# Score products of the first two head pairs from operands written in place, with a changed order of the start

## The chip, the cores and the metric
One NeuronCore of a Trainium2 chip runs one program. Its engines work in parallel, each in the order of its own queue: PE (matrix products; PEld is its weight load), DVE (vector), ACT (scalar and activation functions), POOL (GpSimd) and SP (which here only issues DMAs). The metric is the device time of one execution in microseconds (us); less is better.

## The reference, cut to what matters
The input is q, k, v of 4 batches x 8 heads x 576 positions x 64 values, and the weights of two feed-forward layers. The attention output (2304 rows of 512) goes through a layer of 8 experts, of which each row takes one, and then through a dense layer of 2048 hidden units.

```python
q_rot, k_rot = (rotate(q), rotate(k))
scores = scale * np.matmul(q_rot, k_rot.transpose(0, 1, 3, 2))
scores = scores - np.max(scores, axis=-1, keepdims=True)
attn = np.exp(scores)
attn = attn / (np.sum(attn, axis=-1, keepdims=True) + 1e-09)
return np.matmul(attn, v).astype(np.float32)
...
h = x @ w_in
r = np.maximum(h, 0.0)
g = r * r
return (g @ w_out).astype(np.float32)
```

## The kernel before, in words
**Stages.** `attention` takes the 32 heads as 16 pairs (P = 0 to 15); then come the experts and the dense layer. Two heads of 64 values fill the 128 partitions: head j of a pair lies on partitions 64j to 64j+63. A pair's q and k come in one load of 1.28 MB (`load`, L176, tile `qk`, two buffers, so the load of pair P+2 waits until the last reader of pair P's buffer is done). `rotate` (L189) turns them in place with three operations over 1280 columns: two products with tables (`times`, L392) and one sum (`plus`, L388). For pair 0 it is done in two halves, k (n = 0) and q (n = 1).

**Splitting.** The products run in a rounded 32-bit format, so each operand is split: `high` (L195) writes the rounded part `hi` on ACT, `low` (L202) the rest `lo` by a subtraction (on POOL unless told otherwise; `minus` is L384). Score = hi·hi + lo·hi + hi·lo. `stack_up` (L212) rearranges by DMA: for each head j, `kZ` holds the head's k high part twice, on both halves of the partitions, `qZ` holds its q high part above its q low part, and `QH[P % 2][j]` holds the q high part on the head's own partitions, with zeros on the other 64 (written once, L150). One product of `kZ` and `qZ` over 128 partitions then gives hi·hi + lo·hi.

**Scores.** A pair has nine score tiles s = 0 to 8, in the order 2, 8, 4, 1, 0, 5, 7, 3, 6. Tiles 0 to 7 are 128 queries of one head (j = s // 4) against 576 keys, in two halves u of 288 columns; tile 8 holds the last 64 queries of both heads. `scores` (L228) makes tiles 0 to 7 of 4 products (2 at L241, 2 at L243) and tile 8 of 6, into one of two PSUM buffers `ps`. `smax` (L250) takes the maximum on DVE, `sexp` (L253) the exponential and its sum on ACT, which frees the buffer. `turn` (L261) transposes the exponentials on PE into one of four buffers `pp`, `turned` (L278) copies them out on DVE or ACT, `values` (L296) multiplies with v, and `project` and `finish` scale and gather.

**Order.** The order of the work on every queue is written out by hand: `at(t, f)` puts a step into a heap under a planned time t, and the steps are issued in order of t, after all of `prepare` (L140). The planned times only order the queues; an engine waits for what it needs. The offsets `OFF` (L103) are added to 15.954 P. For pair 1 score 2 stands at 31.6, its exponential at 33.4 and score 4 at 34.7; for pair 0 exponentials 5, 7, 3 and 6 stand at 25.7, 26.4, 29.4 and 30.1. For pair 2 the three operations of `rotate` on POOL stand at 20.6, 23.6 and 26.5, `high` on ACT at 32.1, `low` on POOL at 33.6 and `stack_up` at 36.7; for pair 3 `load` stands at 21.9 and `rotate` at 36.6 to 42.4. `prepare` itself holds the loads, the clearing of buffers, all of pair 0's and pair 1's rotating and splitting, 16 products on PE that nobody reads (`warm`, L162), and both pairs' `stack_up`.

Of the kernel before, what the change touches and what calls it, by code (L numbers as in the profile page):

```python
# [10 lines left out]
F32 = mybir.dt.float32  # L11
F32R = mybir.dt.float32r
I32 = mybir.dt.int32
U32 = mybir.dt.uint32
AF = mybir.ActivationFunctionType
# [6 lines left out]
B, H, S, D = 4, 8, 576, 64  # L22
# [35 lines left out]
def shape_constants():  # L58
# [27 lines left out]
    for b in range(B):  # L86
        for c in range(4):
# [15 lines left out]
OFF = dict(pair=15.954, load=-26.0, v=8.0, rope=-11.279, hi=0.235, lo=1.675, z=4.815,  # L103
           S=[21.118, 20.135, 15.671, 27.85, 18.735, 24.184, 28.378, 24.712, 17.071],
           max=[21.846, 20.96, 16.399, 28.578, 19.463, 24.912, 29.183, 25.517, 18.084],
           exp=[22.666, 21.951, 17.479, 29.363, 20.248, 25.697, 30.078, 26.412, 18.869],
           un=[32.589, 32.153, 35.217, 38.036, 36.617, 23.748, 28.906, 37.6, 35.653, 34.253, 33.817],
           out=[33.418, 34.148, 36.917, 39.025, 37.411, 29.788, 32.958, 38.405, 36.294, 35.538, 34.643],
           av=[41.194, 44.969], x=[46.747, 47.789], pj=54.426, fin=58.03)
# [3 lines left out]
def attention(tc, rope, ident, qk, v, w_gate, xd, on_batch, later):  # L113
    nc = tc.nc
    stack = contextlib.ExitStack()
    pool = lambda name, **kw: stack.enter_context(tc.tile_pool(name=name, bufs=1, reuse_waits="tile", **kw))
    ldp, cp, wp = pool("ld"), pool("ac"), pool("aw")
# [7 lines left out]
    QH = [[cp.tile([128, 512], F32R, name=f"QH{i}{j}") for j in range(2)] for i in range(2)]  # L125

    SS = [cp.tile([128, 9, 2], F32, name=f"ss{i}") for i in range(6)]
    T = {}
    sched = []

    def at(t, f):
        heapq.heappush(sched, (round(t, 3), len(T["n"]), f))
        T["n"].append(0)
# [3 lines left out]
    def ppt(name, shape=(128, 512)):  # L137
        return psa.tile(list(shape), F32, name=name, tag="pp", bufs=4)

    def prepare():  # L140
        nc.scalar.dma_start(out=TB[:, :, 0], in_=rope)
        load(0)
        load(1)
        for t in Xs:
            nc.gpsimd.memset(t[:, 576:640], 0.0)
        for t in SS:
            nc.gpsimd.memset(t[:, :, 1:2], 1e-9)
        for two in QH:
            for j in range(2):
                nc.gpsimd.memset(two[j][64 - 64 * j:128 - 64 * j].bitcast(F32), 0.0)  # L150
        nc.gpsimd.memset(R, 0.0)
        for r in range(2):
            d = slice(64 * r, 64 * r + 64)
            nc.gpsimd.tensor_copy(R[d, :, r, 0:64], ident[d, d].unsqueeze(1).broadcast_to([64, 4, 64]))
        for o, lo, hi in ((0, 64, 640), (576, 0, 64)):
            nc.scalar.activation(TB[:, :, 1, o:o + hi - lo], TB[:, :, 0, lo:hi], AF.Copy, scale=0.125)
        for n in range(2):
            rotate(0, n, nc.vector)
            high(0, n)
        w = ppt("warm")  # L160
        for i in range(16):
            nc.tensor.matmul(w, T["hi", 0][:, 0, 0:128], T["hi", 0][:, 0, 0:512], start=True, stop=True)  # L162
        for n in range(2):
            low(0, n, nc.vector)
            stack_up(0, n)
        load(2)
        rotate(1, None, nc.vector)
        high(1)
        low(1)
        load_v(0)  # L170
        for r in range(2):
            nc.sync.dma_start(out=R[64 * r:64 * r + 64, :, r, 64:72], in_=w_gate.rearrange("(g r d) e -> r d g e", r=2, d=64)[r])
        later()
        stack_up(1)

    def load(P):  # L176
        t = T["qk", P] = ldp.tile([128, 2, 2, 640], F32, name="qk", tag="qk", bufs=2)
        src = qk[P].rearrange("p (w n c) -> p w n c", w=2, n=2)
        if P == 0:
            for n in range(2):  # L180
                nc.sync.dma_start(out=t[:, :, n], in_=src[:, :, n])
        else:
            nc.sync.dma_start(out=t, in_=src)

    def load_v(P):
        V = T["V", P] = ldp.tile([128, 2, 5, 64], F32, name="V", tag="V", bufs=2)
        nc.sync.dma_start(out=V, in_=v[P].rearrange("p (h c d) -> p h c d", h=2, c=5))

    def rotate(P, n, eng, step=None):  # L189
        x, a = T["qk", P], slice(0, 2) if n is None else slice(n, n + 1)  # L190
        for i, (f, o, y) in enumerate(((times, 0, TB[:, 0, a]), (times, 1, TB[:, 1, a]), (plus, 0, x[:, 1, a]))):
            if step in (None, i):
                f(eng, x[:, o, a], x[:, o, a], y)

    def high(P, n=None):  # L195

        if ("hi", P) not in T:
            T["hi", P] = wp.tile([128, 2, 640], F32R, name="XH", tag="XH", bufs=2)
        a = slice(0, 2) if n is None else slice(n, n + 1)
        nc.scalar.activation(T["hi", P][:, a], T["qk", P][:, 0, a], AF.Copy)  # L200

    def low(P, n=None, eng=None):  # L202
        if ("lo", P) not in T:
            T["lo", P] = wp.tile([128, 2, 640], F32R, name="XL", tag="XL", bufs=2)
        a = slice(0, 2) if n is None else slice(n, n + 1)
        args = T["lo", P][:, a], T["qk", P][:, 0, a], T["hi", P][:, a].bitcast(F32)
        if eng is None:
            nc.gpsimd.tensor_sub(*args)
        else:
            minus(eng, *args)  # L210

    def stack_up(P, n=None):  # L212

        h, l = T["hi", P].bitcast(F32), T["lo", P].bitcast(F32)
        for j in range(2):
            r = slice(64 * j, 64 * j + 64)
            q = nc.scalar if P == 0 and j == 1 else nc.sync
            if n != 1:
                Z = T["kZ", 2 * P + j] = wp.tile([128, 640], F32R, name="kZ", tag="kZ", bufs=4)
                for i in range(2):  # L220
                    q.dma_start(out=Z[64 * i:64 * i + 64].bitcast(F32), in_=h[r, 0])
            if n != 0:
                Z = T["qZ", 2 * P + j] = wp.tile([128, 640], F32R, name="qZ", tag="qZ", bufs=4)
                q.dma_start(out=Z[0:64].bitcast(F32), in_=h[r, 1])
                q.dma_start(out=QH[P % 2][j][r].bitcast(F32), in_=h[r, 1, 0:512])
                q.dma_start(out=Z[64:128].bitcast(F32), in_=l[r, 1])

    def scores(P, s):  # L228

        t = T["S", P, s] = ps.tile([128, 2, 512], F32, name="ps", tag="ps", bufs=2)  # L230
        if s < 8:
            j, c = divmod(s, 4)
            todo, qs, qh = [j], slice(c * 128, c * 128 + 128), QH[P % 2][j]
            qh = qh[:, qs]
        else:
            todo, qs, qh = [0, 1], slice(512, 640), T["hi", P][:, 1, 512:640]
        k0 = 0 if s in (4, 5, 6, 7) else 64
        for i, j in enumerate(todo):
            Q1, K1 = T["qZ", 2 * P + j], T["kZ", 2 * P + j]
            for u in range(2):  # L240
                nc.tensor.matmul(t[:, u, 0:288], Q1[:, qs], K1[:, k0 + 288 * u:k0 + 288 * u + 288], start=i == 0, stop=False)  # L241
        for u in range(2):
            nc.tensor.matmul(t[:, u, 0:288], qh, T["lo", P][:, 0, k0 + 288 * u:k0 + 288 * u + 288], start=False, stop=True)  # L243
# [98 lines left out]
    def route(P, t=None):  # L342
        t = OFF["pair"] * P + OFF["fin"] + .02 if t is None else t
        d = next(T["route", P], None)
        if d is not None:
            t += d if P + 1 < NPAIR else 0
            at(t, lambda: route(P, t))

    prepare()
    for P in range(NPAIR):  # L350
        def on(o, f, *args):
            at(OFF["pair"] * P + o, lambda: f(*args))

        if P > 2:
            on(OFF["load"], load, P)
        if P > 0:
            on(OFF["v"], load_v, P)
        if P > 1:
            for i in range(3):
                on(OFF["rope"] + 2.93 * i, rotate, P, None, nc.gpsimd, i)  # L360
            on(OFF["hi"], high, P)
            on(OFF["lo"], low, P)
            on(OFF["z"], stack_up, P)
        for s in range(9):
            on(OFF["S"][s], scores, P, s)
            on(OFF["max"][s], smax, P, s)
            on(OFF["exp"][s], sexp, P, s)
        for un, o, o2 in zip(UNITS, OFF["un"], OFF["out"]):
            on(o, turn, P, un)
            on(o2, turned, P, un)  # L370
        for u in range(2):
            on(OFF["av"][u], values, P, u)
            on(OFF["x"][u], gathered, P, u)
        on(OFF["pj"], project, P)
        on(OFF["fin"], finish, P)
        if P % 4 == 3:
            on(OFF["fin"] + .02, route, P)
# [5 lines left out]
def minus(v, out, a, b):  # L383
    v.tensor_tensor(out=out, in0=a, in1=b, op=ALU.subtract)  # L384
# [565 lines left out]
def body(tc, a, cols):  # L950
    nc = tc.nc
    stack = contextlib.ExitStack()
    with stack:
# [12 lines left out]
        with tc.manual_schedule():  # L966
            attention(tc, a["rope"], ident, a["qk"], a["v"], a["moe_w_gate"], xd,
                      R.batch, lambda: nc.sync.dma_start(out=consts, in_=a["consts"])).close()
# [75 lines left out]
```

## Time and profile before

| what | us |
|---|---|
| median of 3 runs | 1008.9 |
| lowest and highest run | 1007.31, 1009.38 |
| the profiled execution | 1009.21 |
| its span, first to last instruction | 1007.4 |
| PE busy in the span | 973.7 |
| DVE, ACT, POOL busy | 533.0, 429.4, 264.6 |

The profiled execution took 1.8 us more than its span and 0.3 us more than the median. In the rows times are from the start of the span. The granted clock is TensorE's, 1.00 being 2.4 GHz and 0.50 being 1.2 GHz; matmuls are pipelined, so the length of one is not its cost, and the spacing of their starts is.

### The profile page before, as it was taken

What the parts mean: (1) busy time and instruction counts of PE and PEld (TensorE: products, weight loads), DVE (VectorE), ACT (ScalarE), POOL (GpSimd) and SP (SyncE); (2) the same over time, 40 slices, a digit from 0 to 9 for tenths busy, and PEclk for the clock granted to TensorE, in tenths of its full rate; (3) what the DMA queues carried; (4) which work ended last, traced back from release to release, by engine and by line L of the source; (5) the groups of instructions that cost most, each with busy time, mean ns of one, the idle gap of its engine ahead of it and who ended that gap; (6) DMA issues with size and microseconds to landing.
All of it is one profiled execution on the core that took longest, in us unless ns stands there. A gap on an engine that the chain in (4) does not pass through costs nothing. (4 is left out here: it accounts for less than half of the span.)

```text
span 1007.4 us, 15649 instructions
## 1 busy us (share of the span) xinstructions
PE 973.7 (97%) x5632; PEld 836.6 (83%) x5632; DVE 533.0 (53%) x901; ACT 429.4 (43%) x841; POOL 264.6 (26%) x195
## 2 busy tenths in 40 slices
PE   4999999999997999999999999999999999999998
PEld 3787888787876788888878789999999999999997
DVE  5677777777766355566565449722322323323222
ACT  3666666666632233344455347632222322322222
POOL 3786887796212111123243300000000000000000
PEclk8999999999999899999999999999999999999999
DMA  9876867785354744247365514110010010100000
GB/s 284 235 197 198 233 203 205 226 214 142 98 187 133 239 136 129 85 126 233 127 245 175 186 54 160 40 63 1 1 64 1 12 52 1 63 1 1 32 1 32
DMA packets 43409, 121.21 MB, mean 120 GB/s; under 512 B 5936, under 2 KB 5936, under 8 KB 40880
## 3 DMA queue, kind: packets, MB, share of 16 engines
q1 hardware_dynamic: 38544, 104.95, 33.6%
q0 software_dynamic: 4096, 13.63, 4.1%
q10 hardware_dynamic: 672, 1.44, 0.6%
q8 instruction: 47, 0.77, 0.3%
q14 instruction: 50, 0.41, 0.1%
HBM read 79.90 MB, written 14.94 MB: 94 GB/s over the span
## 5 line engine op out<-in xcount | busy, mean ns | idle before, releaser
L876 PE MATMUL h<-xs,Wi 128*128 128x384 f32 x1152 | 217.3, 337 | 0.7 <-ACT xs L867 0.7
L897 PE MATMUL o<-Wo,gs 128*128 128x512 f32 x864 | 216.0, 394 | 0.0
L876 PEld LDWEIGHTS h<-xs,Wi 128*128 128x128 f32 x1152 | 204.7, 188 | 9.0 <-ACT xs L867 0.9
L897 PEld LDWEIGHTS o<-Wo,gs 128*128 128x128 f32 x864 | 159.9, 188 | 29.3
L885 DVE SCALAR_TENSOR_TENSOR g<-h,r 128x384 f32<-128x384 f32 x80 | 44.6, 558 | 193.0 <-ACT r L881 193.0
L258 ACT ACTIVATE e<-ps,mx 128x576 f32<-128x576 f32 x144 | 106.3, 740 | 82.3 <-DVE mx L251 82.2
L251 DVE TENSOR_REDUCE mx<-ps 128x1 f32<-128x576 f32 x144 | 105.8, 753 | 62.7 <-PE ps L243 62.7
L881 ACT ACTIVATE r<-h 128x384 f32<-128x384 f32 x96 | 47.2, 491 | 212.9 <-PE h L876 212.7
L687 PE MATMUL p_h<-W,xs 128*128 128x512 f32 x504 | 123.2, 400 | 5.3 <-ACTq L720 2.6
L709 PE MATMUL p_y<-W,hh 128*128 128x512 f32 x504 | 121.1, 395 | 2.1 <-DVE W L665 0.9
L687 PEld LDWEIGHTS p_h<-W,xs 128*128 128x128 f32 x504 | 94.7, 192 | 25.8 <-ACTq L720 2.8
L709 PEld LDWEIGHTS p_y<-W,hh 128*128 128x128 f32 x504 | 93.0, 188 | 21.9 <-DVE W L665 1.2
L887 DVE TENSOR_TENSOR gs<-g,gs 128x384 fp32r<-128x384 f32 x96 | 53.5, 558 | 60.1 <-ACT gs L886 60.0
L276 PE MATMUL pp<-ident,e 128*128 128x128 f32 x640 | 85.2, 273 | 0.0
L241 PE MATMUL ps<-kZ,qZ 128*128 128x288 f32 x320 | 78.7, 336 | 6.0 <-DMA qZ<-XL 3.1
L392 POOL TENSOR_TENSOR qk<-qk,TB 128x1280 f32<-128x1280 f32 x28 | 81.4, 2926 | 1.1 <-DMA qk<-in_qk_dram 1.1
L276 PEld LDWEIGHTS pp<-ident,e 128*128 128x128 f32 x640 | 74.9, 141 | 0.5 <-issue 0.4
L886 ACT ACTIVATE gs<-g 128x384 fp32r<-128x384 f32 x96 | 50.5, 526 | 50.5 <-DVE g L885 50.0
L303 PE MATMUL av<-eT,V 128*64 128x288 f32 x512 | 69.1, 412 | 0.0
L241 PEld LDWEIGHTS ps<-kZ,qZ 128*128 128x128 f32 x320 | 49.7, 195 | 22.6 <-ACT X L306 6.1
L292 DVE COPY eT<-pp 128x512 f32<-128x512 f32 x96 | 64.3, 684 | 4.1 <-PE pp L276 2.0
L713 POOL DMA_INDIRECT yd<-yo,idx x21 | 20.9, 993 | 160.1 <-DVE yo L712 153.0
(160 smaller groups left out, 1088.2 us busy)
## 6 DMA issues: line engine op xcount, KB each, us to landing
raw<-in_moe_w_dram SPq DMA_DIRECT2D x44, 512.0 KB, 3.8
qk<-in_qk_dram SPq DMA_DIRECT2D x15, 1280.0 KB, 6.7
kZ<-XH SPq DMA_DIRECT2D x62, 160.0 KB, 2.9
w<-in_moe_w_in_dram SPq DMA_DIRECT2D x8, 1024.0 KB, 5.2
w<-in_moe_w_out_dram SPq DMA_DIRECT2D x8, 1024.0 KB
V<-in_v_dram SPq DMA_DIRECT2D x16, 320.0 KB, 3.3
qZ<-XH SPq DMA_DIRECT2D x31, 160.0 KB, 3.9
qZ<-XL SPq DMA_DIRECT2D x31, 160.0 KB, 2.5
```

Source lines behind the costliest of these rows:

```text
L241: nc.tensor.matmul(t[:, u, 0:288], Q1[:, qs], K1[:, k0 + 288 * u:k0 + 288 * u + 288], start=i == 0, stop=False)
L251: nc.vector.tensor_reduce(small("mx", P, 9)[:, s:s + 1], T["S", P, s][:, :, 0:288], axis=AX.XY, op=ALU.max, negate=True)
L258: nc.scalar.activation(ed.rearrange("p (u n) -> p u n", u=2), T["S", P, s][:, :, 0:288], AF.Exp, bias=T["mx", P][:, s:s + 1], accum_out=SS ...
L276: nc.tensor.transpose(t[:, c * 128:c * 128 + 128], src, ident)
L292: nc.vector.tensor_copy(o, i)
L303: nc.tensor.matmul(t[64 * j:64 * j + 64], V[:, j, kc], eT[:, j, kc, cs] if kc < 4 else eL[:, cs], start=kc == 0, stop=kc == 4)
L392: v.tensor_tensor(out=out, in0=a, in1=b, op=ALU.mult)
L687: nc.tensor.matmul(t[:, 512 * u:512 * u + 512], s[:, a, k], W1[:, b, k, 512 * u:512 * u + 512], start=n == 0, stop=n == 11)
L709: nc.tensor.matmul(t, s[:, a, k], W2[:, b, k], start=n == 0, stop=n == 23)
L876: nc.tensor.matmul(t, W[:, a, k, fs], s[:, c, k], start=n == 0, stop=n == 11)
L887: nc.vector.tensor_sub(gs[:, 1], g, gs[:, 0].bitcast(F32))
L897: nc.tensor.matmul(self.T["o", b][c], gs[:, a, 128 * c:128 * c + 128], W[:, w], start=(f == 0 and n == 0), stop=(f == 15 and n == 2))
```

## The change
For pairs 0 and 1 nothing is stacked by DMA. `direct_high` writes each head's rounded q straight into `QH` (zeros on the other head's partitions), `direct_low` writes its low part into `qZ` on the same partitions, whose other half is cleared once by four new memsets on POOL, and `scores` makes every tile of 6 products over the unstacked `hi` and `lo` (hi·hi, lo·hi, hi·lo, two halves each). For pair 0 it first issues 2 more products per tile into the same buffer, which the next one overwrites. The two unread products use `QH[0][0]` and pair 0's k. The warm products are 14, not 16, and stand before the rotation of pair 0's q. Pair 1's rotation goes from DVE to POOL; its splitting (`second_pair`) stands at 25.75, between pair 0's exponentials 5 and 7 on ACT, with all its subtractions on POOL. Pair 2's rotation on POOL stands at 30.3 to 30.5. The gate's weights and the constants are loaded at 24.0, not in `prepare`.

```diff
--- before.py
+++ after.py
@@ -154,24 +154,49 @@
             nc.gpsimd.tensor_copy(R[d, :, r, 0:64], ident[d, d].unsqueeze(1).broadcast_to([64, 4, 64]))
         for o, lo, hi in ((0, 64, 640), (576, 0, 64)):
             nc.scalar.activation(TB[:, :, 1, o:o + hi - lo], TB[:, :, 0, lo:hi], AF.Copy, scale=0.125)
-        for n in range(2):
-            rotate(0, n, nc.vector)
-            high(0, n)
+        for P in range(2):
+            for j in range(2):
+                Z = T["qZ", 2 * P + j] = wp.tile([128, 640], F32R, name="qZ", tag="qZ", bufs=4)
+                nc.gpsimd.memset(Z[64 - 64 * j:128 - 64 * j, 0:512].bitcast(F32), 0.0)
+        rotate(0, 0, nc.vector)
+        high(0, 0)
         w = ppt("warm")
-        for i in range(16):
+        for i in range(14):
             nc.tensor.matmul(w, T["hi", 0][:, 0, 0:128], T["hi", 0][:, 0, 0:512], start=True, stop=True)
-        for n in range(2):
-            low(0, n, nc.vector)
-            stack_up(0, n)
+        rotate(0, 1, nc.vector)
+        direct_high(0)
+        low(0, 0, nc.vector)
+        direct_low(0, nc.vector)
+        rotate(1, None, nc.gpsimd)
+        load_v(0)
         load(2)
-        rotate(1, None, nc.vector)
-        high(1)
-        low(1)
-        load_v(0)
+
+    def second_pair():
+        high(1, 0)
+        direct_high(1)
+        low(1, 0)
+        direct_low(1, nc.gpsimd)
+
+    def direct_high(P):
+
+
+        x, h = T["qk", P], T["hi", P]
+        for j in range(2):
+            r = slice(64 * j, 64 * j + 64)
+            nc.scalar.activation(QH[P][j][r], x[r, 0, 1, 0:512], AF.Copy)
+        nc.scalar.activation(h[:, 1, 512:640], x[:, 0, 1, 512:640], AF.Copy)
+
+    def direct_low(P, eng):
+        x = T["qk", P]
+        for j in range(2):
+            r = slice(64 * j, 64 * j + 64)
+            minus(eng, T["qZ", 2 * P + j][r, 0:512], x[r, 0, 1, 0:512], QH[P][j][r].bitcast(F32))
+        minus(nc.gpsimd, T["lo", P][:, 1, 512:640], x[:, 0, 1, 512:640], T["hi", P][:, 1, 512:640].bitcast(F32))
+
+    def gate_weights():
         for r in range(2):
             nc.sync.dma_start(out=R[64 * r:64 * r + 64, :, r, 64:72], in_=w_gate.rearrange("(g r d) e -> r d g e", r=2, d=64)[r])
         later()
-        stack_up(1)
 
     def load(P):
         t = T["qk", P] = ldp.tile([128, 2, 2, 640], F32, name="qk", tag="qk", bufs=2)
@@ -235,6 +260,16 @@
         else:
             todo, qs, qh = [0, 1], slice(512, 640), T["hi", P][:, 1, 512:640]
         k0 = 0 if s in (4, 5, 6, 7) else 64
+        if P == 0:
+            for u in range(2):
+                nc.tensor.matmul(t[:, u, 0:288], QH[0][0][:, 0:128], T["hi", 0][:, 0, 0:288], start=True, stop=True)
+        if P < 2:
+            H, L = T["hi", P], T["lo", P]
+            ql = L[:, 1, 512:640] if s == 8 else T["qZ", 2 * P + j][:, qs]
+            for i, (q1, k1) in enumerate(((qh, H), (ql, H), (qh, L))):
+                for u in range(2):
+                    nc.tensor.matmul(t[:, u, 0:288], q1, k1[:, 0, k0 + 288 * u:k0 + 288 * u + 288], start=i == 0, stop=i == 2)
+            return
         for i, j in enumerate(todo):
             Q1, K1 = T["qZ", 2 * P + j], T["kZ", 2 * P + j]
             for u in range(2):
@@ -347,6 +382,8 @@
             at(t, lambda: route(P, t))
 
     prepare()
+    at(24.0, gate_weights)
+    at(25.75, second_pair)
     for P in range(NPAIR):
         def on(o, f, *args):
             at(OFF["pair"] * P + o, lambda: f(*args))
@@ -357,7 +394,7 @@
             on(OFF["v"], load_v, P)
         if P > 1:
             for i in range(3):
-                on(OFF["rope"] + 2.93 * i, rotate, P, None, nc.gpsimd, i)
+                on(OFF["rope"] + 2.93 * i if P > 2 else 30.3 + .1 * i - OFF["pair"] * P, rotate, P, None, nc.gpsimd, i)
             on(OFF["hi"], high, P)
             on(OFF["lo"], low, P)
             on(OFF["z"], stack_up, P)
```

## Rows read from the trace of the kernel before

**Rows 1.** Windows of 50 us: engine busy us, granted clock, DMA share, GB/s.
```profile
0.00:50.00 50.00, 34.08 (x191) 27.61 (x192) 29.12 (x43) 24.52 (x50) 27.70 (x29) 0.90 0.88 260
50.00:100.00 50.00, 50.00 (x395) 41.15 (x394) 37.41 (x79) 33.54 (x77) 35.26 (x13) 1.00 0.72 198
...
200.00:250.00 50.00, 49.98 (x392) 40.86 (x391) 38.34 (x83) 32.50 (x78) 40.76 (x26) 1.00 0.65 169
```

**Rows 2.** Timeline: start us, length us, engine, line, operation, shapes, [idle before <-releaser].
```profile
10.21 6.34 PE L162 MATMUL warm<-XH 128*128 128x512 f32 x16 [10.21 <-ACT XH L200]
...
11.63 1.71 DVE L384 TENSOR_TENSOR XL<-qk,XH 128x640 fp32r<-128x640 f32 x2
11.75 0.74 ACT L200 ACTIVATE XH<-qk 128x640 fp32r<-128x640 f32 x1 [1.59 <-DVE qk L388]
...
19.47 0.85 PE L241 MATMUL ps<-kZ,qZ 128*128 128x288 f32 x2 [2.93 <-DMA qZ<-XL]
```

**Rows 3.** Windows of 1 us around the first scores.
```profile
18.00:19.00 1.00, 0.00 (x0) 0.00 (x0) 0.00 (x0) 0.97 (x1) 0.00 (x0) 0.90 1.09 263
...
29.00:30.00 1.00, 0.59 (x4) 0.36 (x3) 1.00 (x2) 0.29 (x1) 1.00 (x1) 0.98 1.06 252
```

**Rows 4.** Timeline, one turn through a score buffer of pair 0.
```profile
30.60 0.54 PE L241 MATMUL ps<-kZ,qZ 128*128 128x288 f32 x2 [1.00 <-ACT e L258]
...
31.44 1.48 DVE L251 TENSOR_REDUCE mx<-ps 128x1 f32<-128x576 f32 x2 [1.05 <-PE ps L243]
...
32.23 0.74 ACT L258 ACTIVATE e<-ps,mx 128x576 f32<-128x576 f32 x1 [0.96 <-DVE mx L251]
...
33.12 0.53 PE L241 MATMUL ps<-kZ,qZ 128*128 128x288 f32 x2 [0.89 <-ACT e L258]
```

**Rows 5.** Timeline of POOL in the first 38 us.
```profile
1.76 2.24 POOL L150 MEMSET QH<- 64x512 f32 x4
...
23.12 5.78 POOL L392 TENSOR_TENSOR qk<-qk,TB 128x1280 f32<-128x1280 f32 x2 [1.09 <-DMA qk<-in_qk_dram]
...
28.98 2.91 POOL L388 TENSOR_TENSOR qk<-qk 128x1280 f32<-128x1280 f32 x1
...
35.02 2.93 POOL L208 TENSOR_TENSOR XL<-qk,XH 128x1280 fp32r<-128x1280 f32 x1 [3.13 <-DMA V<-in_v_dram]
```

**Rows 6.** Timeline, ACT and PE around the start of pair 1.
```profile
32.96 0.73 ACT L258 ACTIVATE e<-ps,mx 128x576 f32<-128x576 f32 x1
...
33.68 1.27 ACT L200 ACTIVATE XH<-qk 128x1280 fp32r<-128x1280 f32 x1
...
34.84 0.74 ACT L258 ACTIVATE e<-ps,mx 128x576 f32<-128x576 f32 x1
...
35.43 1.04 PE L276 MATMUL pp<-ident,e 128*128 128x128 f32 x8
...
36.22 0.51 PE L241 MATMUL ps<-kZ,qZ 128*128 128x288 f32 x2
```

**Rows 7.** Timeline of PE, products that follow each other without a wait.
```profile
45.17 0.43 PE L241 MATMUL ps<-kZ,qZ 128*128 128x288 f32 x2
...
45.44 0.43 PE L243 MATMUL ps<-XL,QH 128*128 128x288 f32 x2
```

**Rows 8.** Windows of 1 us around two later rises of the clock.
```profile
298.00:299.00 1.00, 0.15 (x1) 0.15 (x1) 0.90 (x5) 0.00 (x0) 0.00 (x0) 0.85 0.93 283
...
302.00:303.00 1.00, 1.00 (x10) 1.00 (x10) 0.86 (x5) 0.00 (x0) 0.00 (x0) 0.94 1.03 399
...
328.00:329.00 1.00, 0.47 (x1) 0.48 (x2) 0.44 (x1) 0.00 (x0) 0.67 (x1) 0.50 0.99 162
...
332.00:333.00 1.00, 1.00 (x4) 0.77 (x4) 0.00 (x0) 0.00 (x0) 0.00 (x0) 0.58 0.93 277
```

**Rows 9.** Timeline of PE, transposes inside the slow stretch of the start.
```profile
26.69 1.06 PE L276 MATMUL pp<-ident,e 128*128 128x128 f32 x4
```

**Rows 10.** DMA issues: KB each, median us from issue to landing.
```profile
qk<-in_qk_dram SPq DMA_DIRECT2D x15, 1280.0 KB, 6.7
```

## The prediction

> **What bounds the kernel now.** I read the windows of 50 us first. PE is busy for 34.1 of the first 50 us and practically all the time in the windows behind them [rows 1]. So the attention is bound by PE once it has begun in earnest; a microsecond of PE work added there is added to the end, and a microsecond saved ahead of it comes off, as long as PE stays fed. The timeline of the start shows where the first 50 us lose time: the warm products end at 16.55, the first score begins at 19.47, and what ended the last 2.93 us of that wait was a DMA of the stacking [rows 2]. The windows of 1 us show the second loss: the granted clock falls from 2.4 to 1.2 GHz at about 18.8, 2.3 us after PE went idle, and is back at 29.0 [rows 3]. Then the timeline from 30 to 38 us shows the loop in which pair 0's scores run (product, maximum, exponential, buffer free), and who stands in ACT's queue when pair 1 begins [rows 4, 6]. POOL's timeline shows how early it is with pair 2: its rotation runs from 23.12 to 31.89, and ACT rounds pair 2 at 33.68, 1.8 us later [rows 5, 6]. That small lead is what the change touches.
>
> **The start: a gain of 3.6 us at the first score.** Pair 0's q is rotated at 11.7, where ACT began with it before [rows 2]. From the two lengths on ACT, 0.74 us for 640 columns and 1.27 for 1280 [rows 2, 6], I estimate 0.63 us for 512 columns and 0.3 for 128: `QH` is there at 12.4 and 13.0. DVE's subtractions, at most 0.86 us each [rows 2], end by 14.3. The four new memsets cost POOL 2.24 us, as the same four did [rows 5], and POOL has nothing to do there. So PE is what is late next: its warm products. A product of 288 columns follows the next at 0.27/2 = 0.13 us [rows 7], which makes 512 columns 0.24; two fewer end the issue about 0.5 us earlier, near 15.9. First score: 15.9 instead of 19.47. The clock is up by then, and I expect it to stay, since it stayed up in a window with PE busy for 0.59 of 1 us [rows 3].
>
> **Pair 0's loop.** One buffer's turn at full clock was 0.84 us from product to maximum, 0.79 to the exponential and 0.89 until the next product, 2.52 in all [rows 4]. Four more products add 0.53: 3.05 per two scores. Scores 2, 4, 0, 7 of one buffer start at 15.9, 18.95, 22.0 and 25.0; score 5, behind four transposes, at 23.45, and its exponential runs from 25.6 to 26.4. Now ACT takes pair 1's high parts: 0.74 + 0.63 + 0.63 + 0.3, less some 0.2 of overlap, to 28.5. Exponential 7 starts there instead of at 27.2, frees its buffer at 29.4, score 6 starts, and the last exponential ends at 32.3, against 33.69 before [rows 6]. Pair 1's first score starts at about 30.6 (33.12 before, [rows 4]). So 2.5 to 3.6 us are won up to here.
>
> **POOL's queue, the term that decides.** POOL rotates pair 1 from 13.6 to 22.3 (5.78 + 2.91, [rows 5]), in time. Then its queue holds pair 1's four subtractions, and behind them pair 2's rotation. The first waits for ACT's rounding at 27.15. At 2.93 us per 1280 columns [rows 5] they cost 1.47 + 1.17 + 1.17 + 0.3 = 4.1 us and end at 31.3. Pair 2's rotation follows with 8.7 us to 40.1, where it ended at 31.89. But `high(2)` was not moved: at a planned 32.1 it stands in ACT's queue behind pair 0's last exponential and ahead of all of pair 1's. ACT reaches it at 32.3 and waits 7.8 us. Behind it are pair 1's exponentials, which free the score buffers, and ACT's copies of pair 0's transposes. PE can still issue pair 1's scores 2 and 8 and sixteen transposes, to about 34.1, and then stands before score 4, whose buffer waits for exponential 2. ACT ends `high(2)` 1.16 us (its spacing before, [rows 6]) after 40.1, at 41.3; 0.89 us later score 4 starts, at 42.2. Before it was 36.22 [rows 6]. **Term 1: +6.0 us.** Bounds: 4.8, if a subtraction over 64 partitions costs only 0.56 us as a memset there does [rows 5]; 6.6, if each of ACT's four parts costs the 0.74 us of 640 columns [rows 2]. I take the row of the same operation.
>
> **Extra products: term 2, +1.85 us.** From score 4 on, seven of pair 1's scores have two products more, 14 x 0.132 [rows 7], on a PE that is the bound. None if all fall into gaps of the restart; no row shows such gaps in this stretch, so I take the whole.
>
> **The clock after the stop: term 3, +2.0 us.** PE is idle from 34 to 42, much longer than the pause after which the clock fell [rows 2, 3]. How long it stays low I take from two later places: a dense stretch that began at 298.85 brought it back at about 302.1, one that began at 328.5 at about 332.8 [rows 8], 3.2 and 4.3 us. About 4 us at half speed lose 2.0. Bounds: nothing, and 4 if it takes 8 us.
>
> A page's rule would make this longer. The trace has the clock rise at 29.0 in a stretch whose dense part holds four transposes, at 26.69 [rows 9]. The Trainium skill, TensorE: Matmul & The Clock Gate, section Part 4: PE-mode transpose, says that transposes don't count as busy in the way that products do; by it the restart, half transposes, would stay slow, which is rival 2.
>
> **What costs nothing.** Saved stacking DMAs of pairs 0 and 1: nobody waits for them any more, so their whole worth is in the early start. Pair 3's load now waits for POOL's last subtraction at 31.3 and blocks SP's queue until then (before it was issued near 28); with 6.7 us to land [rows 10] it is there at 38, and POOL wants it only at about 44. Behind it on SP are the gate's weights and the constants, wanted after 55. Pair 2's stacking ends some 6 us later, like its user. DVE loses 3 operations and gains none that is waited for.
>
> **Sum.** 6.0 + 1.85 + 2.0 = 9.9, call it 10. What follows is fed by PE, and the next stages start from the attention's end, so I pass it on whole. The profiled execution took 1009.2, so 1019.2 for it; it is 0.3 above the median, so against the median 1008.9 + 10 = **1018.9 us**. The forecast's own bounds are 1008.9 + 4.8 = 1013.7 and 1008.9 + 6.6 + 1.85 + 4 = 1021.4.
>
> **Rival 1, not slower: the stop doesn't happen.** It decides at one point: pair 2's rotation has to be done when ACT comes to `high(2)` at 32.3. Then exponential 2 of pair 1 runs at 32.5, PE is busy to 34.1 without a wait and score 4 starts there, 2.1 us before 36.22. If the extra products fall into gaps, 1008.9 - 2.1 = 1006.8, faster; if they cost their 1.85, 1008.6, no change. For it speaks that before the rotation was ahead of ACT; against it that it would have to end 7.8 us earlier than POOL's prices allow, with nothing on POOL or ACT to overtake in a queue. 0.09: faster 0.05, no change 0.04.
>
> **Rival 2: the clock stays low through the mixed restart.** By transposes that don't count, PE would be slow until the first long run of products with v: before, 5.74 us from 36.22, with the extra products 7.0, lost once more: 1008.9 + 6.0 + 1.85 + 7.0 = 1023.8. Against it: the rise at 29.0 with transposes close before [rows 3, 9]. 0.08.
>
> **Rival 3: the unread products don't do what they are put there for**, and the clock falls between pair 0's scores. A turn of the loop with eight products at half clock is longer by 8 x 0.132, 1.05 us, four turns some 4 us: 1008.9 + 10 + 4 = 1022.9. Against it: the clock held at lower use [rows 3]. 0.08. A start no earlier than 19.47, for a reason that I don't see, ends in the same place.
>
> **How the numbers follow.** Forecast 0.75, rivals 0.09, 0.08, 0.08. A measurement of this kernel can tell about 0.2% (2.0 us). The forecast lies above that even at its lower bound, as do rivals 2 and 3: slower 0.91, same 0.04, faster 0.05. The range 1014.8 to 1022.9 holds nearly all of the forecast (its lowest corner needs all three terms at their least) and rival 3; rival 2 and rival 1 stay out, 0.17, and a little of the forecast.
>
> **What would show it.** In the changed profile: the first score near 15.9 with the clock at 1.00 through 30 us; POOL's rotation of pair 2 from about 31 to 40; ACT idle some 8 us before `high(2)`, released by POOL; PE idle from about 34 to 42, released by ACT; the clock at 0.50 for some 4 us from 42 on; and everything behind 60 us about 10 us later, stage by stage. The prediction is wrong if ACT does not wait at `high(2)`, if PE has other work to issue in the wait, or if the stages behind absorb the shift.

## The result, and the profile after

The changed kernel takes **1019.15 us** (median of 4 runs, 1018.04 to 1019.87) against 1009.02 for the kernel before beside it: ratio **1.0103**, interval 1.0085 to 1.0120. The forecast was 1018.9, the range 1014.8 to 1022.9. The profiled execution took 1019.25 with a span of 1017.5; its counterpart of before took 1009.21, so the profiles differ by 10.0.

I read the views in the order of the prediction. The windows of 50 us, with the columns of [rows 1]:

```profile
0.00:50.00 50.00, 29.87 (x165) 27.15 (x166) 21.08 (x34) 21.35 (x44) 37.01 (x39) 0.90 0.51 168
50.00:100.00 50.00, 50.00 (x395) 41.13 (x394) 35.75 (x68) 33.05 (x77) 33.67 (x13) 1.00 0.69 189
...
200.00:250.00 50.00, 49.97 (x394) 40.86 (x392) 37.58 (x81) 32.85 (x78) 40.95 (x23) 1.00 0.74 201
```

PE is busy for 29.87 of the first 50 us where it was 34.08, POOL for 37.01 where it was 27.70, and from 50 us on both traces look alike: the whole difference is made in the first 50 us, as in [rows 1] the whole loss was. The timeline of PE says where:

```profile
16.05 0.42 PE L265 MATMUL ps<-XH,QH 128*128 128x288 f32 x2
...
29.41 0.73 PE L265 MATMUL ps<-XH,QH 128*128 128x288 f32 x2 [1.52 <-ACT e L293]
...
31.45 0.83 PE L271 MATMUL ps<-XH,QH 128*128 128x288 f32 x2
...
34.68 1.03 PE L311 MATMUL pp<-ident,e 128*128 128x128 f32 x8
...
42.60 0.85 PE L271 MATMUL ps<-XH,QH 128*128 128x288 f32 x2 [6.89 <-ACT e L293]
...
301.67 1.64 PE L349 MATMUL pj<-R,X 128*128 128x144 f32 x10
...
308.78 4.57 PE L449 MATMUL p_y<-ident 128*128 128x128 f32 x24 [1.35 <-DVE rk L429]
```

The first score starts at 16.05 with its two unread products (L265), 3.4 us earlier than in [rows 2]; pair 1's first score at 31.45, still 1.7 us earlier than in [rows 4]. Then PE issues what it has, ends eight transposes at 35.71, and stands for 6.89 us until pair 1's score 4 at 42.60, which was at 36.22 in [rows 6]. The wait is put down to an exponential on ACT. ACT's own timeline shows what held that up:

```profile
32.41 0.74 ACT L293 ACTIVATE e<-ps,mx 128x576 f32<-128x576 f32 x1 [2.34 <-DVE mx L286]
...
40.56 1.27 ACT L225 ACTIVATE XH<-qk 128x1280 fp32r<-128x1280 f32 x1 [7.32 <-POOL qk L425]
41.74 0.72 ACT L293 ACTIVATE e<-ps,mx 128x576 f32<-128x576 f32 x1
```

Between pair 0's last exponential and pair 1's first stands the rounding of pair 2 (`high(2)`), and it waits 7.32 us for POOL. The exponential behind it waits for nothing more itself; it starts when the rounding lets it. So one goes on to POOL:

```profile
13.92 5.81 POOL L429 TENSOR_TENSOR qk<-qk,TB 128x1280 f32<-128x1280 f32 x2
19.81 2.92 POOL L425 TENSOR_TENSOR qk<-qk 128x1280 f32<-128x1280 f32 x1
27.21 1.55 POOL L233 TENSOR_TENSOR XL<-qk,XH 128x640 fp32r<-128x640 f32 x1 [4.48 <-ACT XH L225]
28.71 2.61 POOL L421 TENSOR_TENSOR qZ<-qk,QH 64x512 fp32r<-64x512 f32 x2
31.40 0.45 POOL L421 TENSOR_TENSOR XL<-qk,XH 128x128 fp32r<-128x128 f32 x1
31.81 5.76 POOL L429 TENSOR_TENSOR qk<-qk,TB 128x1280 f32<-128x1280 f32 x2
37.65 2.88 POOL L425 TENSOR_TENSOR qk<-qk 128x1280 f32<-128x1280 f32 x1
```

POOL is done with pair 1's rotation at 22.7, idles 4.48 us for ACT, subtracts until 31.8, and only then rotates pair 2, to 40.5; in [rows 5] that rotation ended at 31.9. Last the windows of 1 us, for the clock (the number after POOL's is the granted clock):

```profile
28.00:29.00 1.00, 0.00 (x0) 0.00 (x0) 0.68 (x1) 0.98 (x3) 1.00 (x2) 1.00 0.00 0
29.00:30.00 1.00, 0.59 (x3) 0.59 (x4) 0.00 (x0) 1.00 (x4) 0.97 (x1) 0.78 0.00 0
...
39.00:40.00 1.00, 0.00 (x0) 0.00 (x0) 0.00 (x0) 0.00 (x0) 1.00 (x1) 0.90 0.00 0
...
43.00:44.00 1.00, 1.00 (x6) 1.00 (x5) 0.00 (x0) 1.00 (x4) 1.00 (x1) 0.50 0.94 207
...
46.00:47.00 1.00, 1.00 (x7) 1.00 (x7) 0.69 (x1) 0.56 (x2) 1.00 (x1) 0.69 0.97 222
```

A mean of 0.78 over a microsecond that begins at 1.00 and ends at 0.50 puts the fall at 29.56: 0.15 us after PE took up work again behind a pause of 1.5 us. The clock is back at 33, falls again at 39.8 in the stop, and is back at about 46.6: 4.0 us of PE's work from 42.60 run at half speed.

A good place to measure the first part of the kernel by itself is the last pair's projection. In the kernel before it starts 9.93 us earlier than the 301.67 above:

```profile
291.74 1.64 PE L314 MATMUL pj<-R,X 128*128 128x144 f32 x10
```

### The profile page after: what moved, and what is told of

Read it like the earlier page. It is cut to its first block, busy times and chain, and to the rows that moved or that the text cites. A ratio compares the mean times of both kernels' runs of the same rounds, so it can differ in the third digit from the quotient of the medians.

```text
span 1017.5 us, 15727 instructions
## 1 busy us (share of the span) xinstructions
PE 978.9 (96%) x5680; PEld 843.7 (83%) x5680; DVE 529.9 (52%) x899; ACT 430.4 (42%) x846; POOL 277.3 (27%) x206
## 5 line engine op out<-in xcount | busy, mean ns | idle before, releaser
L429 POOL TENSOR_TENSOR qk<-qk,TB 128x1280 f32<-128x1280 f32 x30 | 87.1, 2922 | 0.0
L276 PE MATMUL ps<-kZ,qZ 128*128 128x288 f32 x280 | 66.7, 327 | 0.3
L737 ACT ACTIVATE hh<-p_t 128x512 fp32r<-128x512 f32 x42 | 22.8, 596 | 79.7 <-PE p_t L736 77.9
```

The costliest lines, as they stand in the source:

```text
L429: v.tensor_tensor(out=out, in0=a, in1=b, op=ALU.mult)
```

## The experiments

Most kernels are the changed kernel with one edit; the ratio is always to the kernel before, run on the same chip (its median was 1007.6 to 1008.3 beside e1 to e10). "Last projection" is the start of pair 15's projection in the profile, 291.74 before and 301.67 after. It leaves out the later stages, which vary by some us from run to run. "First score" is the start of pair 0's first score tile, 19.47 before. It moves by itself, from 15.00 to 16.27, as the warm products end sooner or later, and what waits for the work behind it moves with it; each profile is one execution. Where a run's early start is part of a gain, the text says so.

| kernel | median, us | ratio, interval | first score | last projection |
|---|---|---|---|---|
| changed | 1019.15 | 1.0103, 1.0085 to 1.0120 | 16.05 | 301.67 |
| e1 pair 1's subtractions on DVE | 1015.28 | 1.0073, 1.0059 to 1.0087 | 16.14 | 297.88 |
| e2 rotation of pair 2 where it was | 1014.17 | 1.0063, 1.0049 to 1.0077 | 15.38 | 296.85 |
| e3 unread products in pair 1 too | 1018.63 | 1.0109, 1.0091 to 1.0127 | 16.00 | 303.39 |
| e4 PE busy in the stop | 1015.85 | 1.0078, 1.0064 to 1.0092 | 15.00 | 298.96 |
| e5 no unread products | 1017.16 | 1.0093, 1.0078 to 1.0109 | 16.07 | 301.16 |
| e6 three subtractions on DVE | 1017.23 | 1.0096, 1.0078 to 1.0113 | 15.17 | 299.04 |
| e7 rounding later in ACT's queue | 1011.76 | 1.0046, 1.0031 to 1.0062 | 15.23 | 295.36 |
| e8 pair 1 stacked | 1008.35 | 1.0008, 0.9998 to 1.0017 | 15.72 | 292.22 |
| e9 stacked, rounding later | 1006.21 | 0.9987, 0.9978 to 0.9996 | 16.27 | 289.86 |
| e10 e9 without unread products | 1005.46 | **0.9979**, 0.9969 to 0.9988 | 15.77 | 288.83 |

**e1: pair 1's subtractions on DVE**, so that POOL can go on to pair 2's rotation at once.

```
-        low(1, 0)
-        direct_low(1, nc.gpsimd)
+        low(1, 0, nc.vector)
+        direct_low(1, nc.vector)
...
-        minus(nc.gpsimd, T["lo", P][:, 1, 512:640], ...
+        minus(nc.gpsimd if P == 0 else eng, T["lo", P][:, 1, 512:640], ...
```

> Pair 1's four subtractions go from POOL to DVE; all else as in the changed kernel. Theory (ACT's wait at pair 2's rounding is the loss): POOL has only pair 2's rotation left behind pair 1's, so it runs from about 22.8 to 31.5, ACT's wait of 7.3 us is gone, pair 1's score 4 starts at about 35.7 instead of 42.6, PE never stops and keeps its clock there; left are the extra products, 1.85, less 0.5 of earlier start: about 1010.3 us, 9 below the changed kernel. Rival A (the extra products and a slow clock at the start are the loss, the wait only shadows them): at most 2 us below the changed kernel. Rival B (pair 2 or 3 comes late by its load or its stacking, since SP is held until the subtractions are done): PE waits for the stacking of pair 2 near 58 us instead, and little is won.

The wait at the rounding is gone: it runs at 35.83, straight behind two exponentials, and POOL is done at 32.1. But the last projection came forward by only 3.79 us where I had expected some 9, for a new stop stands in front of it: PE is idle from 31.96 to 35.27, with the clock down since 29.6. DVE's subtractions made it: the maxima of pair 0's last two scores stand behind them in DVE's queue, and ACT's exponential waits for those. POOL's timeline, then DVE's and ACT's, then the view of the tile `qZ` on DVE (duration shortest/median/longest in ns):

```profile
22.81 5.83 POOL L429 TENSOR_TENSOR qk<-qk,TB 128x1280 f32<-128x1280 f32 x2
28.72 3.37 POOL L425 TENSOR_TENSOR qk<-qk 128x1280 f32<-128x1280 f32 x1
```
```profile
27.32 2.00 DVE L421 TENSOR_TENSOR XL<-qk,XH 128x640 fp32r<-128x640 f32 x1
29.25 4.11 DVE L421 TENSOR_TENSOR qZ<-qk,QH 64x512 fp32r<-64x512 f32 x2
...
33.59 1.42 DVE L286 TENSOR_REDUCE mx<-ps 128x1 f32<-128x576 f32 x2
...
34.38 0.74 ACT L293 ACTIVATE e<-ps,mx 128x576 f32<-128x576 f32 x1 [4.93 <-DVE mx L286]
```
```profile
L421 DVE TENSOR_TENSOR qZ<-qk,QH x2: 690/2038/3386, 29.2 to 32.7; 64x512 fp32r<-64x512 f32 x2
```

Two subtractions of the same shape took 0.69 and 3.39 us. The long one began while POOL's sum ran and ended at 32.64, 0.55 after that sum's end at 32.09; the one before it, begun while POOL's second product ran, ended at 29.32, 0.68 after that product's end at 28.64. Each lasted until POOL was done, and then about its own length; and POOL's sum, 2.9 us elsewhere, took 3.37 with DVE's subtraction at work until 29.32. The two engines took turns, an instruction at a time. The Trainium skill (SBUF — State Buffer, section Who interferes with whom) says that a DVE instruction with two inputs in SBUF contends with a GpSimd instruction that reads SBUF, and calls the pair of ports that the two share an exclusive lock. These rows agree: the 3.39 us ended only behind POOL's sum.

**e6: the control for that**: the same, but the 128-column subtraction stays on POOL ahead of the rotation (the last two lines of e1's edit left out), so that DVE's three begin before POOL has anything to do.

> As the run with all of pair 1's subtractions on DVE, but the last one, 128 columns, is left on POOL ahead of pair 2's rotation, so that POOL stands idle until 28.6 while DVE works. Theory of contention (DVE's operations from SBUF to SBUF are slow, 2 us, only while POOL runs): the first two subtractions take 0.8 and 0.7 us again, the third is slow where POOL's rotation has begun. Rival (DVE is slow for another reason, such as what ACT writes at that time): all three take 2 us. For the stop: rotation 29.1 to 37.9 on POOL, ACT waits at pair 2's rounding until 37.9, pair 1's score 4 starts near 40, the last projection at about 299 (301.67 changed).

The timelines of DVE, POOL and PE:

```profile
26.34 0.82 DVE L421 TENSOR_TENSOR XL<-qk,XH 128x640 fp32r<-128x640 f32 x1
27.08 1.39 DVE L421 TENSOR_TENSOR qZ<-qk,QH 64x512 fp32r<-64x512 f32 x2
...
27.90 0.89 POOL L421 TENSOR_TENSOR XL<-qk,XH 128x128 fp32r<-128x128 f32 x1 [4.90 <-ACT XH L187]
...
39.58 0.85 PE L271 MATMUL ps<-XH,QH 128*128 128x288 f32 x2 [5.79 <-ACT e L293]
```

Begun beside an idle POOL the same three took 0.82 and twice 0.70 us, as pair 0's do, against 2.00 and 4.11 in e1. Here POOL was the one to wait: its 128-column subtraction, begun while DVE's last one ran, took 0.89 us where it took 0.45 in the changed kernel. POOL's rotation starts at 28.75 instead of 31.81, the rounding at 37.54, score 4 at 39.58, each 3.0 us earlier: score 4 comes earlier by what POOL is early. 0.9 us of that is not the edit's: this run's first score was early, and ACT rounded pair 1 at 25.53 instead of 26.40. PE's stop itself shrinks only from 6.89 to 5.79 us, as PE's work ahead of it was earlier too.

**e2: pair 2's rotation at its old place**, ahead of the subtractions in POOL's queue.

```
-                on(OFF["rope"] + 2.93 * i if P > 2 else 30.3 + .1 * i - OFF["pair"] * P, rotate, P, None, nc.gpsimd, i)
+                on(OFF["rope"] + 2.93 * i, rotate, P, None, nc.gpsimd, i)
```

> Only pair 2's rotation is put back to its planned times of before (20.6, 23.6, 26.5), so that two of its three operations stand ahead of pair 1's subtractions on POOL. Theory: rotation's products 22.8 to 28.5, subtractions to 33.3, sum to 36.2; ACT waits some 3 us at pair 2's rounding instead of 7.3, pair 1's score 4 starts near 38.3: about 4.5 us below the changed kernel, 1014.5. Rival A: no change beyond 0.5 us. If the subtractions' own lateness counts as much (pair 1's first scores then wait for them to 31.5 and 33.3), the gain is smaller, 2 to 3 us.

The timelines of ACT and PE:

```profile
35.96 1.27 ACT L225 ACTIVATE XH<-qk 128x1280 fp32r<-128x1280 f32 x1 [4.23 <-POOL qk L425]
...
38.00 0.53 PE L271 MATMUL ps<-XH,QH 128*128 128x288 f32 x2 [3.21 <-ACT e L293]
```

About as expected (1014.5; 1014.17 measured). POOL, idle before, takes the two products of the rotation at 22.6, and only the sum comes behind the subtractions, 33.02 to 35.9. ACT's wait shrinks from 7.32 to 4.23, PE's from 6.89 to 3.21, score 4 starts 4.6 us earlier, the last projection 4.8.

**e7: the rounding later in ACT's queue**, behind pair 1's exponentials 2, 8 and 4 and four copies; POOL's work stays in the changed kernel's order. What hangs on the rounding moves with it.

```
+            on(OFF["load"] + (.5 if P == 4 else 0), load, P)
...
+            on(OFF["hi"] + (5.75 if P == 2 else 0), high, P)
+            on(OFF["lo"] + (4.4 if P == 2 else 0), low, P)
+            on(OFF["z"] + (1.35 if P == 2 else 0), stack_up, P)
```

(The first of pair 3's three operations of `rotate` is planned 1.6 later too.)

> Only the place of pair 2's rounding in ACT's queue is changed: planned at 37.9 instead of 32.1, behind pair 1's exponentials 2, 8 and 4, with what hangs on it (its subtraction, its stacking, pair 3's first rotation step, pair 4's load) moved just behind it; POOL's rotation of pair 2 ends as late as before, near 40.5. Theory (the loss is made by what stands behind the rounding in ACT's queue, not by pair 2's lateness as such): score 4 starts at about 34.5 instead of 42.6, ACT waits about 3 us instead of 7.3, PE stops 2 to 4 us, then pair 3's rotation, which ends at 53.5, makes a second, shorter wait; the last projection starts at 296 to 298. Rival B (pair 2's lateness itself is the bound): no change, 301.7.

The timelines of PE and ACT:

```profile
33.31 0.51 PE L271 MATMUL ps<-XH,QH 128*128 128x288 f32 x2
...
39.83 1.27 ACT L225 ACTIVATE XH<-qk 128x1280 fp32r<-128x1280 f32 x1 [2.74 <-POOL qk L425]
...
41.87 0.85 PE L271 MATMUL ps<-XH,QH 128*128 128x288 f32 x2 [3.32 <-ACT e L293]
```

Pair 2 is rounded at 39.83, hardly earlier than the 40.56 of the changed kernel (0.7 us, by this run's early first score); yet score 4 runs at 33.31 without a wait, and the last projection is 6.31 us earlier. Of the 9.93 us lost, some 5.5 were not lateness of pair 2 but of what stood behind its rounding. What is left is a shorter stop of the same kind, and the extra products.

**e3: term 2 doubled.** The two unread products of pair 0's score tiles are made for pair 1's too.

```
-        if P == 0:
+        if P < 2:
             for u in range(2):
-                nc.tensor.matmul(t[:, u, 0:288], QH[0][0][:, 0:128], T["hi", 0][:, 0, 0:288], ...
+                nc.tensor.matmul(t[:, u, 0:288], QH[P][0][:, 0:128], T["hi", P][:, 0, 0:288], ...
```

> Two unread products also ahead of each of pair 1's nine scores: doubles the second term. Theory (PE is the bound from pair 1's third score on, a product of 288 columns costs 0.132 us): the seven scores behind the stop cost 7 x 2 x 0.132 = 1.85 us, the two ahead of it nothing: 1021.0 us. If extra products fall into gaps, no change: 1019.1.

PE's timeline, the last projection and the routing behind it:

```profile
303.39 1.64 PE L349 MATMUL pj<-R,X 128*128 128x144 f32 x10
...
310.49 2.94 PE L449 MATMUL p_y<-ident 128*128 128x128 f32 x24 [1.36 <-DVE rk L429]
```

The total doesn't resolve it: the ratios of e3 and of the changed kernel overlap. The stage does: score 4 starts at 42.58, as in the changed kernel, and from there to the first pair's projection it is 24.52 us against 22.82, for 14 more products (the last projection: 1.72 later). I expected 1.85. Most of why the total hides it is in the second row. In this profile the 24 products behind the last pair (`keep_warm`, the identity matrix with itself, which nobody reads) took 2.94 us, in the profile of the changed kernel 4.57, at half clock in part: 1.6 us that come or go with the run.

**e4: term 3 taken away.** 28 products of 512 columns, which nobody reads, put into the stop to keep PE busy.

```
+    def unread():
+        for i in range(28):
+            nc.tensor.matmul(T["PT", 0, (0, 0)], T["hi", 1][:, 0, 0:128], T["hi", 1][:, 0, 0:512], start=True, stop=True)
...
+    at(34.6, unread)
```

> 28 unread products of 512 columns (28 x 0.216 = 6 us) on PE in the stop between pair 1's second and third score, so that the clock has no reason to fall; they end about 1 us before the stop does. Theory: the wait stays at its length, the clock stays at 1.00, and the 3.7 us at half clock behind the stop are won back in half: 1.8 us below the changed kernel, 1017.3. If the slow clock behind the stop costs nothing (other engines set the pace of the restart): 1019.1. If the unread products delay the stop's end: above that.

PE's timeline, and under it a window of 1 us:

```profile
10.28 4.88 PE L165 MATMUL warm<-XH 128*128 128x512 f32 x14 [10.28 <-ACT XH L225]
...
33.08 6.63 PE L390 MATMUL pp<-XH 128*128 128x512 f32 x28
...
41.73 0.53 PE L271 MATMUL ps<-XH,QH 128*128 128x288 f32 x2 [2.02 <-ACT e L293]
```
```profile
42.00:43.00 1.00, 1.00 (x10) 1.00 (x10) 0.17 (x1) 1.00 (x4) 1.00 (x1) 1.00 0.78 172
```

The clock is at 1.00 right after the stop, where it was 0.50. From score 4 to the first projection it is 20.94 us instead of 22.82: **1.88 us** for the clock. The other 0.87 of the 2.71 us by which the last projection came earlier was there at score 4 already (41.73 against 42.60). It is not the edit's: in this run the warm products took 4.88 us instead of 6.19, and the first score started at 15.00 instead of 16.05. (The granted clock is 1.00 through the warm products in both views, so they don't show why.) I had expected a median of 1017.3; 0.87 of the 1.5 us between that and 1015.85 is this early start.

**e5: no unread products in pair 0**, the lines `if P == 0:` and below left out.

> The unread products of pair 0 are left out. Measured at the start of the last pair's projection (291.74 us before, 301.67 changed), since the stages behind it vary by up to 3 us from run to run. Theory, if the clock stays up without them: three turns of pair 0's loop up to exponential 5 are shorter by 2 x 0.132 us each, POOL's chain to pair 2's rounding starts 0.8 us earlier, so the last projection starts at about 300.9. If the unread products hold the clock: it falls between 19 and 25 us, each turn is longer by 6 x 0.12 us, and the last projection starts at 302.5 to 304.

Windows of 1 us, and under them a row of PE's timeline:

```profile
21.00:22.00 1.00, 0.48 (x3) 0.48 (x4) 0.39 (x1) 1.00 (x3) 1.00 (x1) 1.00 0.00 0
...
29.00:30.00 1.00, 1.00 (x9) 0.98 (x8) 0.53 (x1) 0.04 (x1) 1.00 (x1) 0.79 0.00 0
```
```profile
28.37 0.53 PE L269 MATMUL ps<-XH,QH 128*128 128x288 f32 x2 [1.79 <-ACT e L291]
```

The clock holds at 1.00 between pair 0's scores without them, with PE busy for 0.48 of a microsecond, and falls at the same time as with them, at 29.6, behind the pause in which ACT rounds pair 1; here PE had been at work again since 28.37. They hold nothing here. Without them score 4 starts 1.04 us earlier, at 41.56; the clock comes back at 46.6 all the same, and 0.5 us is left at the last projection.

**e8 to e10: a version that keeps the early start.** If the reading is right, the start is worth its 2.5 to 3.6 us as soon as POOL is not late and ACT doesn't wait. e8 leaves pair 0 as changed, but stacks pair 1 as before (four products a tile), with the products of its rotation on DVE and pair 2's rotation at its old times:

```
-        rotate(1, None, nc.gpsimd)
+        rotate(1, None, nc.vector, 0)
+        rotate(1, None, nc.vector, 1)
+        rotate(1, None, nc.gpsimd, 2)
...
     def second_pair():
-        high(1, 0)
-        direct_high(1)
-        low(1, 0)
-        direct_low(1, nc.gpsimd)
+        high(1)
+        low(1)
+        stack_up(1)
...
-        if P < 2:
+        if P == 0:
...
-    at(25.75, second_pair)
+    at(18.9, second_pair)
```

(e2's edit belongs to it too, and two of the four clearings of `qZ` are left out.)

> Pair 0 as in the changed kernel; pair 1 stacked by DMA with 4 products per tile as before, its rotation's two products on DVE while it idles (13.7 to 16.6) and the sum on POOL, its rounding on ACT in the idle 1.1 us ahead of exponential 4, pair 2's rotation at its planned times of before. Theory: nothing is added to POOL or ACT ahead of pair 2's rounding, which waits under 2 us; no extra products in pair 1; the early start is kept in part: score 4 of pair 1 at about 35, last projection at about 290.5, 1 us earlier than before; time 1007.5. If the start's gain needs pair 1's change too: as before or slower.

The timelines of ACT and PE, and windows of 1 us:

```profile
33.00 1.27 ACT L226 ACTIVATE XH<-qk 128x1280 fp32r<-128x1280 f32 x1 [1.94 <-POOL qk L426]
...
35.04 0.54 PE L277 MATMUL ps<-kZ,qZ 128*128 128x288 f32 x2 [2.00 <-ACT e L294]
```
```profile
35.00:36.00 1.00, 0.96 (x5) 0.94 (x6) 0.00 (x0) 1.00 (x3) 1.00 (x1) 0.72 0.70 167
36.00:37.00 1.00, 1.00 (x7) 1.00 (x6) 0.76 (x1) 0.80 (x4) 1.00 (x1) 0.50 0.94 200
...
38.00:39.00 1.00, 1.00 (x7) 0.98 (x6) 0.73 (x2) 0.21 (x1) 1.00 (x1) 0.57 0.94 205
```

It can't be told from the kernel before, and misses what was expected of it by 1.7 us at the last projection: POOL is now only 1.94 us late for the rounding, but that is enough for a stop of 2.00 us, and behind it the clock is down from 35.4 to 38.9. So e9 moves the rounding behind pair 1's exponentials 2 and 8 as well:

```
+            on(OFF["hi"] + (2.86 if P == 2 else 0), high, P)
+            on(OFF["lo"] + (1.52 if P == 2 else 0), low, P)
```

> The run with pair 1 stacked, and pair 2's rounding planned at 34.97 instead of 32.14, behind pair 1's exponentials 2 and 8 in ACT's queue (its subtraction just behind it). Theory: in that run ACT waited 1.9 us at the rounding and PE then stood from 33.0 to 35.0 and lost its clock for 3 us; with two exponentials ahead of the rounding nothing waits, PE does not stop, score 4 of pair 1 starts near 33.5 (36.22 before): last projection 289.3 to 290 (291.74 before, 292.22 in that run), time 2 us below before, ratio 0.998. Rival: the early start is worth nothing in the end, because PE then waits for pair 2 (its stacking needs the rounding): last projection at 291.5 or later.

PE's timeline, and a window of 1 us:

```profile
33.06 0.51 PE L277 MATMUL ps<-kZ,qZ 128*128 128x288 f32 x2
...
36.74 0.54 PE L277 MATMUL ps<-kZ,qZ 128*128 128x288 f32 x2 [1.06 <-ACT e L294]
```
```profile
36.00:37.00 1.00, 0.26 (x2) 0.26 (x3) 0.10 (x1) 1.00 (x3) 1.00 (x1) 1.00 0.40 89
```

Score 4 at 33.06 without a wait, one wait of 1.06 us left, the clock at 1.00 through it, and the last projection 1.88 us earlier than in the kernel before. e10 leaves out the unread products as well:

> The same without pair 0's unread products. Theory: the clock held without them up to 29 us in the run that left them out, and here no second_pair on ACT makes the pause in which it fell; pair 0's four turns are shorter by 1.1 us, so the last projection starts 0.5 to 1.1 us earlier than in the run beside it, 288.3 to 289.3, ratio 0.997. If they hold the clock after all: 2 to 4 us later than the run beside it.

PE's timeline:

```profile
288.83 1.64 PE L348 MATMUL pj<-R,X 128*128 128x144 f32 x10
```

The last projection starts another 1.03 us earlier; half of that was there at the first score already (15.77 against 16.27 in e9). With 0.9979, interval 0.9969 to 0.9988, e10 is faster than both kernels, by 0.2% than the one before: the early start is good for 2 us, which the changed kernel loses again, and 10 more, by what it puts into POOL's queue ahead of pair 2's rotation, what that does to ACT's, PE's and the clock, and pair 1's extra products. What the later rounding alone would give the kernel before was not run; there PE has no stop at the rounding and is busy in every microsecond from 34 to 50, so it had little to win.

## Why the prediction was right

**The start.** First score foreseen at 15.9, measured 16.05 (15.00 to 16.27 over all the profiles of kernels with this start, so that a part of the close match is luck). Pair 1's first score foreseen at about 30.6, measured 31.45; the last exponential ends at 33.2 with its readout, foreseen 32.3. This 0.9 us is **the one step that went wrong**: "I expect it to stay, since it stayed up in a window with PE busy for 0.59 of 1 us". Between the scores it did stay. But the prediction's own times held a pause: exponential 7 at 28.5, behind the moved rounding, and the next score at 29.4 (measured 28.54 and 29.41), with nothing for PE from 27.9 on. I hadn't asked what the clock does in it. It fell at 29.56, and the last score of pair 0 ran at half speed; all of the 0.9 us arises behind 29.41 (from that score's start to the end of the last exponential it is 3.83 us here and 2.97 in e2, where the clock stayed up). It cost nothing, as ACT came to `high(2)` and waited for POOL anyway, only 7.3 us instead of 7.8. In e2, e3, e4, e6 and e7 the clock came through nearly the same pause at 1.00; in e1 and e5 it fell at 29.6 as here.

**Term 1, POOL's queue.** Foreseen: subtractions from 27.15 to 31.3, rotation to 40.1, PE stopped from 34.1, score 4 at 42.2, +6.0. Measured: 27.21 to 31.8, 40.5, 35.7, 42.60, +6.38. The two 64-partition subtractions took 1.30 us each instead of the 1.17 that I took by columns from the full-height row; the lower bound, from the memset, was far off. That it is this chain is shown by moving each of its links: POOL 3.0 us earlier brings score 4 3.0 us earlier (e6), pair 2's rotation ahead in POOL's queue 4.6 us (e2), the rounding further back in ACT's queue 9.3 us, with POOL only 0.7 us earlier than it was (e7).

**Term 2, the extra products.** Foreseen +1.85; doubling them costs 1.70 (e3). **Term 3, the clock.** Foreseen +2.0 from about 4 us at half speed; the rows have 4.0 us of it, and taking it away gives 1.88 (e4). 6.38 + 1.70 + 1.88 = 9.96, and the last projection moved by 9.93. The three misses, +0.4, -0.15 and -0.12, cancel in part: that the forecast of 10 is met to 0.1 us is luck, that each term is near is not.

**What was to cost nothing** did: pair 3's load held SP's queue until 32.2, and no engine waited for it or for what stood behind it.

**The rivals.** *Rival 1* named the right point. Once the rotation is done when ACT comes to the rounding, the stop is gone; but that takes another order of POOL's and ACT's work, e9 and e10, and in e8 a rotation 1.94 us late was enough for a stop of 2.00. The change itself was 7.3 us away from it. *Rival 2* falls: the clock was back 4.0 us into the mixed restart, long before the first run of products with v. The rows at 42.60 and after have eight transposes (44.21 to 46.12) in the stretch that raised it. The Trainium skill (TensorE: Matmul & The Clock Gate, section Part 4: PE-mode transpose) says that transposes don't count as busy as products do. That speaks for a slower return than the trace shows; here transposes among products did not keep the clock down. *Rival 3* falls in part. The unread products indeed don't do what they seem to be put there for (e5), but its price, four slow turns of the loop, isn't paid either: the clock needed no help between the scores here.

## What to carry to other kernels

When work moves onto an engine, follow every in-order queue from there to the next consumer: the 4.6 us of subtractions on POOL did no harm themselves, but they made one rounding late, and that rounding stood on ACT ahead of exponentials that had nothing to do with it. A step that may have to wait for another engine belongs behind the independent work of its queue (e7, e9): moving it was worth more than making what it waits for earlier. And judge a change in one stage at the end of that stage: the last projection, with what the first score had moved by itself taken off, resolved 0.5 to 2 us that the total of 1009 us hid.

## What the runs showed that I had not expected

- **DVE and POOL take turns** where DVE subtracts two SBUF tiles while POOL works on SBUF tiles: the subtraction of 0.69 us took 3.39, ending 0.55 us after POOL's instruction (e1). DVE's maximum, which reads PSUM, kept its 0.76 us beside a rotating POOL. Such work, moved from POOL to DVE, isn't safe just because DVE is idle: POOL must be idle too (e6).
- **Short pauses cost the clock in some runs and not in others.** A pause of 1.5 us before 29.41 ended in a fall in the changed kernel, as in e1 and e5; a pause as long, before 28.36, left the clock at 1.00 in e4, as in e2, e3, e6 and e7. The three that fell are those with the latest first scores, 16.05 to 16.14 against 15.00 to 16.00, and all three fell within 0.03 us of 29.57, though in e5 PE was at work again 1.1 us sooner. A stop of 2.0 us cost the clock in e8, one of 1.06 us did not in e9. What decides between the first two groups stays open.
- **The later stages move by themselves**: the same 24 unread products behind the last pair took 4.57 us in one profile and 2.94 in another, 1.6 us, where the lowest and the highest run of the changed kernel lie 1.8 us apart.
